# Row sums of the attention by four products of their own, and the router's logits in a bank of their own

## The chip, the cores and the metric

The kernel runs on one core of one Trainium2 chip. The metric is the device time of one execution in microseconds (us); several executions are timed and the median counts. TensorE (PE) runs matrix products and loads their stationary operand by separate records (PEld). VectorE (DVE), ScalarE (ACT) and GpSimd (POOL) do the element work, SyncE (SP) issues most of the DMA transfers. Each engine works through its own instructions in program order and waits on semaphores where it needs another engine's result.

## The reference

Three layers in float32, cut to what matters:

```python
# attention: batch 8, 8 heads, 576 positions, head size 64, in chunks of 64
scores = scale * np.matmul(q_c, k_c.transpose(0, 1, 2, 4, 3))
scores = scores - np.max(scores, axis=-1, keepdims=True)
attn = np.exp(scores)
attn = attn / (np.sum(attn, axis=-1, keepdims=True) + 1e-09)
out = np.matmul(attn, v_c)          # becomes x: 4608 tokens x 512
# mixture of 8 experts, one expert per token
logits = x @ w_gate                 # 512 x 8
expert_idx = np.argmax(logits, axis=1)
out[mask] = gate_w[mask, None] * (np.maximum(xe @ w1[e], 0.0) @ w2[e])
# a dense layer 512 -> 2048 -> 512 with a piecewise function between
```

## The kernel before

The 4608 tokens are 36 tiles of 128 (NT). **Attention** runs as 42 steps (attention_step, L711), a software pipeline over the tiles: in step i PE does, in this order, scores(i) into s (L456, 8 products), transp(i-1) of the exponentials into t (L464, 4), xtransp(i-3) of the finished rows into tx (L484, 4), pv(i-2), the product of the transposed exponentials with v into ob (L476, 8), logits(i-4) by expert into lt (L544, 4) and by_token(i-5) (L551, 1), which turns the logits so that tokens stand on the partitions. A float32 product of the kind used here leaves two records on PE and two on PEld, a transpose one of each. The products s and pv use 64 columns of the array each, two at a time side by side; logits uses 32; by_token and the transposes use all 128.

v comes with a column of ones behind each head's 64 columns (arrange, L1191), so pv gives 2 x 65 columns per pair of heads, and the 65th is the sum of the exponentials. DVE, per step (vector_work, L487): the maximum mx(i) of s (L500), the subtraction into p(i) (L503), then rd(i-2) from the 65th columns (L516), its reciprocal (L518), and the scaled rows xr(i-2) (L520), which xtransp takes up one step later. ACT: the copy pt of t (L491), the copy xc of tx (L495), the exponential of p (L504), the copy lt of the logits (L529). Between these stand small DVE operations of the router's gate (gate, L553), some DVE and ACT work on the first expert's weights (raw to wt, L106, L109, L112), and, from batch 3 of the gate on, the fetch of the first window of rows for the experts (fetch, L184): POOL scatters the tokens' places into lists (L617), gathers a list (L163) and rows xg (L140), DVE takes their maxima (L100).

The order on PE, DVE, ACT and SP is written out by the code: background work is inserted by a planner that adds up fixed costs per step (slot, spend, clk), which the change leaves alone. POOL's order is left to the scheduler of the framework. PSUM has 8 banks of 512 float32 per partition. In the attention they are: s two, t one, tx one, ob three (one tile, the middle bank shared by the even and the odd tiles' results), la one. The bank la holds the logits by expert (columns 256 to 383), the logits by token and the counts of the gate (acc). The framework puts accesses of different engines to one bank in program order by semaphores.

**Experts** (ffn, L919): 16 windows of up to 512 tokens; per window 8 groups of 12 products h (L932) and 24 products per tile y (L966). In window 0, in which the last tiles' gate work still runs on PE (rest_of_gate), the h groups go round three banks (hs, L914); from window 1 on, once the attention's banks are free, round four. Window 1's rows come by a chain of their own after the last batch was counted: lists, gathers, maxima, halves in float16, DMA transposes into xtw. **The dense layer** (L1089 on) is products without a gap, o (L1145) and h (L1117).

Of the kernel before, what the change touches and what calls it, by code (L numbers as in the profile page):

```python
# [8 lines left out]
F32 = mybir.dt.float32  # L9
# [4 lines left out]
ALU = mybir.AluOpType  # L14
# [4 lines left out]
P = 128  # L19
NT = 36  # L20
# [18 lines left out]
AHEAD = 3  # L39
# [15 lines left out]
def build(ctx, tc, qT, kT, v1, wg, w1, w2, wi, wo, out):  # L55
    nc = tc.nc
    pe, act, dve, pool, sp = nc.tensor, nc.scalar, nc.vector, nc.gpsimd, nc.sync
# [10 lines left out]
    with tc.manual_schedule(engines={E_.PE, E_.Activation, E_.DVE, E_.SP}):  # L68
# [46 lines left out]
        early = rows.enter_context(tc.tile_pool(name="early", bufs=1, side="right"))  # L115
# [238 lines left out]
        with ExitStack() as ph:  # L354
# [5 lines left out]
            ps_o = ph.enter_context(tc.tile_pool(name="ps_o", bufs=1, space=PSUM))  # L360

            kbd = [bd.tile([P, 2, 2, 4, 2, 64], F32, name=f"kbd{i}") for i in range(AHEAD)]
            vbd = [bd.tile([P, 2, 2, 4, 2, 65], F32, name=f"vbd{i}") for i in range(AHEAD)]
            qt = {}

            def clear(t, by, n=slice(0, 2)):
# [39 lines left out]
            pool.memset(ones16, 1.0)  # L406
            zero16 = early.tile([P, GB + 1, E], F16, name="zero16")
            pool.memset(zero16, 0.0)
            tri16 = early.tile([P, P], F16, name="tri16")
            pool.memset(tri16, 1.0)  # L410
            pool.affine_select(out=tri16, in_=tri16, pattern=[[1, P]], base=0, channel_multiplier=-1,
# [33 lines left out]
            for t in xgs:  # L445
                pool.memset(t, 0.0)

            S, Pm, PT, O, X, XR, LG = {}, {}, {}, {}, {}, {}, {}
            xr = [None]

# [9 lines left out]
            def transp(i):  # L460
                p = Pm.pop(i)
                t = ps_t.tile([P, 4, P], F32, name="t", tag="t")
                for hp in range(4):
                    pe.transpose(t[:, hp, :], p[:, hp * P:hp * P + P], ident)  # L464
                PT[i] = t


            ob = ps_o.tile([P, 1536], F32, name="ob")
            obs = [ob[:, 0:684].rearrange("p (a c) -> p a c", c=171)[:, :, 0:130],
                   ob[:, 812:1496].rearrange("p (a c) -> p a c", c=171)[:, :, 41:171]]  # L470

            def pv(i):
                pt, vb, o = PT.pop(i), vbd[i // 2 % AHEAD][:, :, i % 2], obs[i % 2]
                for hp in range(4):
                    for c in range(2):
                        pe.matmul(o[64 * c:64 * c + 64, hp, :], lhsT=pt[:, hp, 64 * c:64 * c + 64], rhs=vb[:, :, hp, c, :],  # L476
                                  start=True, stop=True)
                O[i] = o

            def xtransp(i):  # L480
# [6 lines left out]
            def vector_work(i):  # L487

                if 0 <= i - 1 < NT:
                    pt = mid.tile([P, 4, P], F32, name="pt", tag="pt")  # L490
                    act.activation(out=pt, in_=PT[i - 1], func=AF.Copy)  # L491
                    PT[i - 1] = pt
                if 0 <= i - 3 < NT:
                    xc = xcp.tile([P, 4, P], F32, name="xc", tag="xc")
                    act.activation(out=xc, in_=X[i - 3], func=AF.Copy)  # L495
                    X[i - 3] = xc
                if i < NT:
                    s3 = S.pop(i).rearrange("p (h k) -> p h k", k=64)
                    mx = mid.tile([P, H, 1], F32, name="mx", tag="mx")
                    dve.tensor_reduce(out=mx, in_=s3, axis=AX.X, op=ALU.max)  # L500
                    yield
                    p = mid.tile([P, 512], F32, name="p", tag="p", bufs=3)
                    dve.tensor_tensor(out=p.rearrange("p (h k) -> p h k", k=64), in0=s3, in1=mx.to_broadcast([P, H, 64]), op=ALU.subtract)  # L503
                    act.activation(out=p, in_=p, func=AF.Exp, scale=0.125)  # L504
                    Pm[i] = p
                    spend(1.35, 0.55)
                slot(1.15)
                yield
                j = i - 2
                if 0 <= j < NT:  # L510
                    if j % 2 == 0:
                        xr[0] = xrp.tile([P, 2, D], F32, name="xr", tag="xr")
                    x = XR[j] = xr[0][:, j % 2]
                    o4 = O.pop(j).rearrange("p a (h d) -> p a h d", d=65)
                    rd = mid.tile([P, 4, 2, 1], F32, name="rd", tag="rd")
                    dve.tensor_scalar(out=rd, in0=o4[:, :, :, 64:65], scalar1=1e-9, scalar2=None, op0=ALU.add)  # L516
                    yield
                    dve.reciprocal(out=rd, in_=rd)  # L518
                    yield
                    dve.tensor_tensor(out=x.rearrange("p (a h d) -> p a h d", h=2, d=64), in0=o4[:, :, :, 0:64],  # L520
                                      in1=rd.to_broadcast([P, 4, 2, 64]), op=ALU.mult)
                    if j % 2 == 1:
                        sp.dma_start(out=xd[(j - 1) * P:(j + 1) * P, :].rearrange("(p t) d -> p (t d)", p=P), in_=xr[0].rearrange("p t d -> p (t d)"))
                    spend(0.95, 0.5)
                slot(1.15)
                yield
                if 0 <= i - 4 < NT:
                    lt = xcp.tile([P, P], F32, name="lt", tag="lt")
                    act.activation(out=lt, in_=LT[i - 4], func=AF.Copy)  # L529
                    LT[i - 4] = lt  # L530
                    spend(0.0, 0.65)
                slot(1.15)
                yield
# [5 lines left out]
            def logits(i):  # L539

                xc = X.pop(i)
                lt = LT[i] = la[:, 256:384]
                for dc in range(4):
                    pe.matmul(lt[32 * dc:32 * dc + 32, :], lhsT=wgr[:, dc, :], rhs=xc[:, dc, :], start=True, stop=True)  # L544

# [301 lines left out]
        with ExitStack() as ph:  # L847
# [63 lines left out]
            htp = ph.enter_context(tc.tile_pool(name="htp", bufs=1))  # L911
            ps_h = ph.enter_context(tc.tile_pool(name="ps_h", bufs=1, space=PSUM))
            ps_y = ph.enter_context(tc.tile_pool(name="ps_y", bufs=1, space=PSUM))
            hs = [ps_h.tile([P, 512], F32, name=f"h{i}") for i in range(3)]  # L914

            more_ys = []
            ht = htp.tile([P, 2, 8, 512], F16, name="ht")
# [133 lines left out]
            for w, (r, k, size) in enumerate(windows):  # L1051
                final = w == len(windows) - 1
                if k == 0:
                    ready[1] = max(ready[1], 2 * r + 2)
                    if r > 0:
                        ready[0] = r + 2
                more = w + 1 < len(windows) and windows[w + 1][1] == 0

                def beside(t):
                    if w == 0:  # L1060
                        next(rest_of_gate, None)
                    slot(t)

                def after(n):
                    leave_one()
                    if more and n == 8:
                        ready[1] = 2 * r + 3

                while w not in xts:
                    advance()  # L1070
                if 0 < w and not final:
                    background.insert(0, fetch(w + 1))
                xt, ids, gates, inv = xts.pop(w)
                ffn(r, xt, size, ids, gates, inv, beside, after, final, before_last if final else None)
                if w == 0:
                    now(rest_of_gate)
                    ps_h4 = ph.enter_context(tc.tile_pool(name="ps_h4", bufs=1, space=PSUM, side="right"))
                    hs.insert(0, ps_h4.tile([P, 512], F32, name="h3"))
                    more_ys.append(ps_h4.tile([P, 512], F32, name="y3"))
                    mpool = ctx.enter_context(tc.tile_pool(name="mw", bufs=1, side="right"))  # L1080
                    mlpw = mpool.tile([P, 17, 2048], F16, name="mlpw")
                    background.append(load_mlp())
# [95 lines left out]
def arrange(np, q, k, v, w_gate, w1, w2, w_in, w_out):  # L1178
    c = np.ascontiguousarray

    def tiles(x):
        return x.reshape(8, 8, 9, 64, 64).transpose(0, 2, 1, 3, 4).reshape(NT, 2, 4, 2, 64, 64)

    def pairs(x):
        return c(x.reshape(NT // 2, 2, P, -1).transpose(0, 2, 1, 3)).reshape(NT // 2, P, -1)

    def transposed(x):
        return pairs(tiles(x).transpose(0, 3, 5, 2, 1, 4).reshape(NT, P, 512))

    vt = tiles(v).transpose(0, 3, 4, 2, 1, 5)  # L1190
    v1 = np.concatenate([vt, np.ones(vt.shape[:-1] + (1,), v.dtype)], axis=-1)  # L1191
    a = {"qT": transposed(q), "kT": transposed(k), "v1": pairs(v1.reshape(NT, P, 520)),
         "wg": c(w_gate.reshape(4, P, E).transpose(1, 0, 2)).reshape(P, 4 * E)}
    for i in range(4):
        a[f"w1_{i}"] = c(w1[:, i * P:(i + 1) * P, :]).reshape(E * P, 1024)
        a[f"w2_{i}"] = c(w2.reshape(E, 4, 2, P, D)[:, i].transpose(0, 2, 1, 3)).reshape(E * P, 1024)
    a["w_in"] = c(w_in.reshape(4, P, 2, 1024).transpose(0, 2, 1, 3)).reshape(8, P, 1024)
    a["w_out"] = c(w_out.reshape(8, 2, P, D).transpose(0, 2, 1, 3)).reshape(8, P, 1024)
    if a["w_in"].dtype == np.float64:
        a["w_in"], a["w_out"] = a["w_in"].view(np.int64), a["w_out"].view(np.int64)  # L1200
    return a
```

## Time and profile before

| | us |
|---|---|
| median of 3 runs | 1379.84 (1378.0 to 1382.45) |
| the profiled execution, its own time | 1387.27 |
| its span in the trace | 1385.3 |
| PE busy in the span | 1325.9 (96%) |
| attention, first product to the first product of window 0 | 4.89 to 189.85 |
| window 0, until PE starts window 1 | 189.85 to 233.36 |
| all the rest | 233.36 to 1385.3 |

The profiled execution is 7.4 us above the median. A busy PE is one with a product under way; gaps stand in brackets behind an instruction, with what ended them. "Issue" is a gap that no semaphore explains. The granted clock of PE is 1.00 for 2.4 GHz and 0.50 for 1.2 GHz.

### The profile page before, as it was taken

The numbers are of one execution on the slowest core, as the hardware profiler recorded it, in microseconds if no ns is written. First come the engines' busy times: TensorE is split into PE (matmuls) and PEld (weight loads), VectorE is DVE, ScalarE is ACT, GpSimd is POOL, SyncE is SP. The second block draws the span as 40 slices with busy tenths as digits, with TensorE's granted clock in tenths as the row PEclk, the third lists the DMA queues.
The fourth block names the chain that finished last, engine by engine and source line by source line (L and its number), as shares of the span: only waits on it lengthen the run. The fifth ranks groups of instructions, "written<-read, shape, count | busy, mean of one in ns | idle before, by whom it ended". The sixth has DMA issues, their size and how long they took to land.

```text
span 1385.3 us, 20006 instructions
## 1 busy us (share of the span) xinstructions
PE 1325.9 (96%) x7735; PEld 697.8 (50%) x7735; DVE 766.2 (55%) x1545; ACT 593.9 (43%) x1000; POOL 151.9 (11%) x190
## 2 busy tenths in 40 slices
PE   7888788999999999989999999999999999999998
PEld 5666653445445445555444444444444444444555
DVE  5558655678678777756464270724518064370723
ACT  3446433666666766644242240413315042240522
POOL 3111231221231222310000000000000000000000
PEclk9999899999999999999999999999999999999999
DMA  9989636666667663312111111111110111111000
GB/s 242 286 265 279 161 91 197 206 206 232 192 204 239 174 207 109 98 52 77 31 53 31 62 22 35 35 31 61 31 61 1 31 61 31 54 23 37 22 26 16
DMA packets 123201, 147.99 MB, mean 107 GB/s; under 512 B 89164, under 2 KB 89164, under 8 KB 121056
## 3 DMA queue, kind: packets, MB, share of 16 engines
q1 hardware_dynamic: 115264, 127.40, 32.6%
q0 software_dynamic: 7840, 19.29, 4.1%
q8 instruction: 62, 1.02, 0.3%
q14 instruction: 35, 0.29, 0.1%
HBM read 99.10 MB, written 29.72 MB: 93 GB/s over the span
## 4 chain that ended last, share of the span: by engine, by line
PE 55%; ACT 0%; issue 0%
PE h L1117 27%; PE o L1145 27%; PE y L966 1%; ACT y L954 0%; ACT ot L1138 0%
## 5 line engine op out<-in xcount | busy, mean ns | idle before, releaser
L1117 PE MATMUL h<-xtw,mlpw 128*128 128x512 f16 (+2 forms) x1920 | 375.1, 358 | 0.8 <-ACT y L954 0.8
L1145 PE MATMUL o<-mlpw,gt 128*128 128x512 f16 x1728 | 374.6, 379 | 0.0
L1122 DVE SCALAR_TENSOR_TENSOR q<-r,kf_g 128x512 f32<-128x512 f32 (+2 forms) x160 | 111.7, 698 | 363.7 <-ACT r L1120 363.7
L1117 PEld LDWEIGHTS <-mlpw 128*128 128x128 f16 x1920 | 187.8, 98 | 187.0 <-issue 1.1
L1145 PEld LDWEIGHTS <-gt 128*128 128x128 f16 x1728 | 169.2, 98 | 203.3
L932 PE MATMUL h<-xtw,wt 128*128 128x384 f16 (+2 forms) x1248 | 213.5, 332 | 14.5 <-DMA xtw<-xh 9.9
L966 PE MATMUL y<-wt,ht 128*128 128x512 f16 x960 | 212.2, 383 | 5.6 <-DVEq L994 5.6
L1120 ACT ACTIVATE r<-h,b_g,a_g 128x512 f32<-128x512 f32 (+2 forms) x160 | 117.6, 735 | 184.9 <-PE h L1117 182.4
L932 PEld LDWEIGHTS <-wt 128*128 128x128 f16 x1248 | 122.4, 99 | 103.6 <-DMA xtw<-xh 10.9
L966 PEld LDWEIGHTS <-ht 128*128 128x128 f16 x960 | 94.5, 99 | 120.0 <-issue 9.6
L1138 ACT ACTIVATE ot<-o,io_g 128x512 f32<-128x512 f32 x36 | 24.0, 688 | 289.7 <-PE o L1145 283.6
L1123 DVE SCALAR_TENSOR_TENSOR q<-h,c_g,q 128x512 f32<-128x512 f32 (+2 forms) x160 | 111.7, 698 | 5.7
L1110 DVE TENSOR_TENSOR gt<-q,gt 128x512 f16<-128x512 f32 (+2 forms) x160 | 100.6, 629 | 1.1 <-ACT gt L1109 0.2
L1109 ACT ACTIVATE gt<-q 128x512 f16<-128x512 f32 (+2 forms) x160 | 92.2, 576 | 10.2 <-DVE q L1123 10.2
L112 DVE SCALAR_TENSOR_TENSOR wt<-raw,s_w,wt 128x1024 f16<-128x1024 f32 x64 | 79.4, 1278 | 8.5 <-ACT wt L109 8.5
L109 ACT ACTIVATE wt<-raw,s_w 128x1024 f16<-128x1024 f32 x64 | 70.5, 1139 | 31.6 <-DVE i_w L89 25.5
L938 DVE SCALAR_TENSOR_TENSOR ht<-h,ht 128x384 f16<-128x384 f32 (+2 forms) x104 | 58.3, 562 | 43.7 <-ACT ht L937 42.1
L106 ACT ACTIVATE wt<-raw 128x1024 bf16<-128x1024 f32 x64 | 66.9, 1048 | 5.1 <-DMA raw<-w 5.1
L937 ACT ACTIVATE ht<-h 128x384 f16<-128x384 f32 (+2 forms) x104 | 50.3, 491 | 43.2 <-PE h L932 37.0
L958 POOL DMA_INDIRECT yd<-y,list x40 | 42.2, 1055 | 92.5 <-ACT y L954 84.8
L456 PE MATMUL s<-kbd,qt 128*64 128x128 f32 x576 | 44.9, 303 | 6.6 <-DMA kbd<-kT 6.5
L476 PE MATMUL ob<-vbd,pt 128*64 128x130 f32 x576 | 45.7, 296 | 5.2 <-issue 5.2
(160 smaller groups left out, 907.4 us busy)
## 6 DMA issues: line engine op xcount, KB each, us to landing
raw<-w SPq DMA_DIRECT2D x64, 512.0 KB
vbd<-v SPq DMA_DIRECT2D x36, 260.0 KB
xd<-xr SPq DMA_DIRECT2D x18, 512.0 KB
xg<-yd SPq DMA_DIRECT2D x36, 256.0 KB
out<-ot SPq DMA_DIRECT2D x36, 256.0 KB
qt<-qT SPq DMA_DIRECT2D x16, 512.0 KB
kbd<-kT SPq DMA_DIRECT2D x32, 256.0 KB
mlpw<-w_in SPq DMA_DIRECT2D x8, 1024.0 KB
```

The costliest lines, as they stand in the source:

```text
L106: act.activation(out=junk, in_=src, func=AF.Square, accum_out=ss)
L109: act.activation(out=hi, in_=src, func=AF.Copy, scale=s)
L112: dve.scalar_tensor_tensor(out=lo, in0=src, scalar=s, in1=hi, op0=ALU.mult, op1=ALU.subtract)
L932: pe.matmul(h[:, 0:N], lhsT=wa[:, a, wc:wc + P], rhs=xt[:, 4 * b + dc, 0:N], start=n == 0, stop=n == 11)
L966: pe.matmul(ys[t], lhsT=ht[:, a, f, c0 + t * P:c0 + (t + 1) * P], rhs=wb[:, b, f * D:(f + 1) * D], start=f == 0 and n == 0, stop=f == 7 an ...
L1109: act.activation(out=gt[:, 0, f, 0:N], in_=q, func=AF.Copy)
L1110: dve.tensor_tensor(out=gt[:, 1, f, 0:N], in0=q, in1=gt[:, 0, f, 0:N], op=ALU.subtract)
L1117: pe.matmul(h[:, 0:N], lhsT=w_in(a, dc, f), rhs=yt[:, 4 * b + dc, 0:N], start=n == 0, stop=n == 11)
L1120: act.activation(out=r, in_=h[:, 0:N], func=AF.Relu, scale=ci["a"], bias=ci["b"])
L1122: dve.scalar_tensor_tensor(out=q, in0=r, scalar=ci["sq"], in1=r, op0=ALU.min, op1=ALU.mult)
L1123: dve.scalar_tensor_tensor(out=q, in0=h[:, 0:N], scalar=ci["c2"], in1=q, op0=ALU.mult, op1=ALU.max)
L1145: pe.matmul(os_[t], lhsT=gt[:, a, f, t * P:(t + 1) * P], rhs=w_out(b, f), start=f == 0 and n == 0, stop=f == 15 and n == 2)
```

## The change

v loses its column of ones: pv has 128 columns per pair of heads, vbd and the input array shrink by 1/65, and ob becomes two tiles of one bank each. The sums come from four new float32 products per tile, right behind pv in the same step: lhsT is the transposed exponentials of two heads (128 x 128), rhs a constant of_head of two columns (ones for the first head's 64 rows, ones for the second's). Their eight results per row lie in a new bank lb, in one of two places by the tile's parity, and rd reads them there. The logits by expert, lt, move from la into lb too; la keeps the logits by token and the counts. The attention's 8 banks are then s two, t, tx, ob two, la, lb; so window 0 of the experts has two h banks where it had three, and four from window 1 on as before. POOL gets three small memsets for of_head at the start.

```diff
-            vbd = [bd.tile([P, 2, 2, 4, 2, 65], F32, name=f"vbd{i}") for i in range(AHEAD)]
+            vbd = [bd.tile([P, 2, 2, 4, 2, 64], F32, name=f"vbd{i}") for i in range(AHEAD)]
...
+            of_head = early.tile([P, 2], F32, name="of_head")
+            pool.memset(of_head, 0.0)
+            for i in range(2):
+                pool.memset(of_head[64 * i:64 * i + 64, i:i + 1], 1.0)
...
-            ob = ps_o.tile([P, 1536], F32, name="ob")
-            obs = [ob[:, 0:684].rearrange("p (a c) -> p a c", c=171)[:, :, 0:130],
-                   ob[:, 812:1496].rearrange("p (a c) -> p a c", c=171)[:, :, 41:171]]
+            obs = [ps_o.tile([P, 4, P], F32, name=f"ob{i}") for i in range(2)]
+
+            lb = ps_l.tile([P, 512], F32, name="lb")
...
                     for c in range(2):
                         pe.matmul(o[64 * c:64 * c + 64, hp, :], lhsT=pt[:, hp, 64 * c:64 * c + 64], rhs=vb[:, :, hp, c, :],
                                   start=True, stop=True)
+                dn = RS[i] = lb[:, P + i % 2 * 8:P + i % 2 * 8 + 8].rearrange("p (a h) -> p a h", h=2)
+                for hp in range(4):
+                    pe.matmul(dn[:, hp, :], lhsT=pt[:, hp, :], rhs=of_head, start=True, stop=True)
                 O[i] = o
...
-                    o4 = O.pop(j).rearrange("p a (h d) -> p a h d", d=65)
+                    o4 = O.pop(j).rearrange("p a (h d) -> p a h d", d=64)
                     rd = mid.tile([P, 4, 2, 1], F32, name="rd", tag="rd")
-                    dve.tensor_scalar(out=rd, in0=o4[:, :, :, 64:65], scalar1=1e-9, scalar2=None, op0=ALU.add)
+                    dve.tensor_scalar(out=rd, in0=RS.pop(j).unsqueeze(3), scalar1=1e-9, scalar2=None, op0=ALU.add)
...
-                lt = LT[i] = la[:, 256:384]
+                lt = LT[i] = lb[:, 0:P]
...
-            hs = [ps_h.tile([P, 512], F32, name=f"h{i}") for i in range(3)]
+            hs = [ps_h.tile([P, 512], F32, name=f"h{i}") for i in range(2)]
...
-                    hs.insert(0, ps_h4.tile([P, 512], F32, name="h3"))
+                    for i in (2, 3):
+                        hs.insert(0, ps_h4.tile([P, 512], F32, name=f"h{i}"))
```

The orders of PE, DVE, ACT and SP stay as they were but for the new products; what changes beside them is what waits for what. In the rows below a name like DVE_49 in the brackets is the semaphore of that engine. On PE, one step in the middle of the attention, before:

```order
L484 MATMUL tx<-ident,xr 128x128 [waits DVE_49,PE_49]
L484 MATMUL tx<-ident,xr 128x128 x3
L476 MATMUL ob<-vbd_132,pt 64x130 [waits DMAHW4_49,DMAHW3_49]
L476 MATMUL ob<-vbd_132,pt 64x130 x7
L544 MATMUL la<-xc,wgr 32x128 [waits Activation_49]
L544 MATMUL la<-xc,wgr 32x128 x3
L551 MATMUL la<-sel_205,lt 128x8
```

and the same step now:

```order
L491 MATMUL tx<-ident,xr 128x128 [waits DVE_49,PE_49]
L491 MATMUL tx<-ident,xr 128x128 x3
L480 MATMUL ob_232<-vbd_132,pt 64x128 [waits DMAHW4_49,DMAHW3_49]
L480 MATMUL ob_232<-vbd_132,pt 64x128 x7
L484 MATMUL lb<-of_head,pt 128x2 [waits Activation_49]
L484 MATMUL lb<-of_head,pt 128x2 x3
L551 MATMUL lb<-xc,wgr 32x128 x4
L558 MATMUL la<-sel_209,lt 128x8
```

Four products stand between pv and the logits, and the wait for ACT's copy of the last tile's logits has moved from the logits to the first of them.

On DVE, the end of a step with a gate's first operations, and the next step's start, before:

```order
L516 TENSOR_SCALAR rd<-ob 128x8 [waits PE_49]
L518 RECIPROCAL rd<-rd 128x8 [waits DVE_49]
L520 TENSOR_TENSOR xr<-ob,rd 128x512 [waits DMAHW3_49,DVE_49]
L557 TENSOR_REDUCE m<-la 128x6 [waits Activation_49]
L560 TENSOR_TENSOR eq<-la,m 128x48 [waits DVE_49]
```

and now:

```order
L523 TENSOR_SCALAR rd<-lb 128x8 [waits PE_49,Activation_49]
L525 RECIPROCAL rd<-rd 128x8 [waits DVE_49]
L527 TENSOR_TENSOR xr<-ob_232,rd 128x512 [waits DMAHW3_49,DVE_49]
L564 TENSOR_REDUCE m<-la 128x6 [waits PE_49]
L567 TENSOR_TENSOR eq<-la,m 128x48 [waits DVE_49]
```

rd waited for the last product of pv; now it waits for the last product of the logits in the same step (they write lb behind the sums) and for ACT's copy of the step before. m, the gate's maximum, waited for ACT's copy lt in the same bank and now waits for PE alone. In turn ACT's copy lt, which waited for PE, waits for DVE's rd.

On ACT, window 0 of the experts, the first copies of h, whose numbers tell the banks, before:

```order
L937 ACTIVATE ht<-h_2428 128x384 [waits PE_49]
L937 ACTIVATE ht<-h_2429 128x384 [waits PE_49]
L937 ACTIVATE ht<-h_2427 128x384 [waits PE_49]
L937 ACTIVATE ht<-h_2428 128x384 [waits PE_49]
L106 ACTIVATE wt,ss<-raw 128x1024 [waits DMAHW7_49]
```

and now:

```order
L944 ACTIVATE ht<-h_2578 128x384 [waits PE_49]
L944 ACTIVATE ht<-h_2577 128x384 [waits PE_49]
L944 ACTIVATE ht<-h_2578 128x384 [waits PE_49]
L944 ACTIVATE ht<-h_2577 128x384 [waits PE_49]
L106 ACTIVATE wt,ss<-raw 128x1024 [waits DMAHW7_49]
```

Every second group of products now goes into a bank that was read just before, where it was every third.

## Rows read from the trace of the kernel before

**Rows 1.** Busy by stage: us; PE, PEld, DVE, ACT, POOL (records); clock, DMA share, GB/s

```profile
29.24:156.16 126.92, 110.61 (x1398) 86.89 (x1399) 80.62 (x230) 66.48 (x134) 26.81 (x28) 0.97 0.94 268
...
233.36:1385.30 1151.94, 1136.16 (x5688) 557.71 (x5688) 621.76 (x1131) 490.49 (x798) 95.31 (x98) 0.99 0.29 85
```

**Rows 2.** Timeline of one attention step: start us, us, engine, line, tile, count

```profile
75.70 1.09 PE L456 MATMUL s<-kbd,qt 128*64 128x128 f32 x16
...
76.72 0.66 PE L464 MATMUL t<-ident,p 128*128 128x128 f32 x4
...
77.11 0.47 PEld L484 LDWEIGHTS tx<-ident,xr 128*128 128x128 f32 x4
...
77.75 1.11 PE L476 MATMUL ob<-vbd,pt 128*64 128x130 f32 x16
...
78.78 0.42 PE L544 MATMUL la<-xc,wgr 128*32 128x128 f32 x8
78.90 0.17 DVE L516 TENSOR_SCALAR rd<-ob 128x8 f32<-128x8 f32 x1 [0.57 <-PE ob L476]
...
79.14 0.30 PEld L551 LDWEIGHTS la<-sel,lt 128*128 128x128 f32 x2 [0.20 <-issue]
...
79.34 0.69 DVE L520 TENSOR_TENSOR xr<-ob,rd 128x512 f32<-128x512 f32 x1
...
79.46 1.09 PE L456 MATMUL s<-kbd,qt 128*64 128x128 f32 x16
```

**Rows 3.** Timeline, float16 weight loads of the gate's count on PEld

```profile
86.59 0.22 PEld L578 LDWEIGHTS <-tri 128*128 128x128 f16 x6
...
86.74 0.22 PEld L580 LDWEIGHTS <-ones 128*128 128x128 f16 x6
```

**Rows 4.** Line L551 and line L484: duration ns min/median/max, first and last start

```profile
L551 PEld LDWEIGHTS la<-sel,lt x72: 186/189/338, 28.6 to 195.6; 128*128 128x128 f32 x72
...
L484 PEld LDWEIGHTS tx<-ident,xr x144: 137/141/231, 20.2 to 190.7; 128*128 128x128 f32 x144
```

**Rows 5.** Waits of PE from 16 to 190 us: in total, times, longest

```profile
PE t L464 <- ACT p L504: 9.5, 5, 6.0
PE ob L476 <- issue: 5.2, 8, 1.0
PE la L544 <- DVE eq L565: 3.4, 1, 3.4
PE tx L484 <- DVE xr L520: 2.4, 3, 1.9
...
PE s L456 <- DMA kbd<-kT: 0.2, 1, 0.2
```

**Rows 6.** Waits of DVE and ACT up to 240 us: in total, times, longest

```profile
DVE xr L520 <- DMA xd<-xr: 5.3, 4, 2.9
...
ACT wt L106 <- DMA raw<-w: 5.1, 2, 4.8
```

**Rows 7.** Timeline of PE: batch 3 counted, and the longest wait, with its neighbours

```profile
134.22 0.24 PE L580 MATMUL la<-oh,ones 128*128 128x32 f16 x4
...
156.16 1.13 PE L456 MATMUL s<-kbd,qt 128*64 128x128 f32 x16
163.32 1.12 PE L464 MATMUL t<-ident,p 128*128 128x128 f32 x4 [6.03 <-ACT p L504]
```

**Rows 8.** Stretches at the lower clock in the attention, columns as in Rows 1

```profile
87.14:90.55 3.41, 3.41 (x24) 2.88 (x22) 3.21 (x12) 2.39 (x5) 0.00 (x0) 0.50 1.01 240
158.82:172.47 13.65, 9.15 (x73) 7.42 (x73) 11.51 (x38) 4.62 (x10) 1.01 (x1) 0.50 0.34 55
```

**Rows 9.** Timeline of PE: window 0 of the experts and the start of window 1

```profile
206.85 4.06 PE L932 MATMUL h<-xtw,wt 128*128 128x384 f16 x24 [1.61 <-DVE ht L938]
210.75 15.70 PE L966 MATMUL y<-wt,ht 128*128 128x512 f16 x72
233.36 17.71 PE L932 MATMUL h<-xtw,wt 128*128 128x384 f16 x96 [6.91 <-DMA xtw<-xh]
```

More of the change, by code (lines that the diff above doesn't have):

```diff
@@ L446, in build @@
                 pool.memset(t, 0.0)
+            RS = {}
             S, Pm, PT, O, X, XR, LG = {}, {}, {}, {}, {}, {}, {}
@@ L519, in vector_work @@
                     yield
-                    dve.tensor_tensor(out=x.rearrange("p (a h d) -> p a h d", h=2, d=64), in0=o4[:, :, :, 0:64],
+                    dve.tensor_tensor(out=x.rearrange("p (a h d) -> p a h d", h=2, d=64), in0=o4,
                                       in1=rd.to_broadcast([P, 4, 2, 64]), op=ALU.mult)
@@ L1190, in arrange @@
     vt = tiles(v).transpose(0, 3, 4, 2, 1, 5)
-    v1 = np.concatenate([vt, np.ones(vt.shape[:-1] + (1,), v.dtype)], axis=-1)
-    a = {"qT": transposed(q), "kT": transposed(k), "v1": pairs(v1.reshape(NT, P, 520)),
+    a = {"qT": transposed(q), "kT": transposed(k), "v1": pairs(vt.reshape(NT, P, 512)),
          "wg": c(w_gate.reshape(4, P, E).transpose(1, 0, 2)).reshape(P, 4 * E)}
```

## Prediction

> **What bounds the kernel now.** I read the busy time by stage first. From 233 us to the end PE is busy 1136.2 of 1151.9 us [rows 1], so whatever the change does there is nothing unless it adds products, and it adds none; a delay made before 233 us is carried to the end whole. The change is in the attention. There, from 29 to 156 us, PE is busy 110.6 of 126.9 us, while DVE has 80.6 and ACT 66.5 [rows 1]: PE is the bound, with gaps. The timeline of one step says the same in another way: scores start at 75.70 and again at 79.46, and the blocks in between follow each other [rows 2]. A step that nothing disturbs is 3.76 us of PE, in order. The DMA engines are busy 0.94 of that stage [rows 1], yet PE waits for a load itself for only 0.2 us after the start [rows 5]; the loads run far enough ahead. So the question is what four more products per tile cost on PE, and how much of it falls into gaps that are there anyway.
>
> **The new products.** Each of the four leaves two loads of 128 x 128 float32 weights, and only two columns to stream behind each, so the loads set the pace. The nearest row is by_token, one product of the same weight shape with 8 columns: its two loads take 0.30 us together [rows 2] and one takes 0.189 [rows 4], so the second starts 0.11 us after the first. The four transposes tx, 128 columns each, give the same: 0.47 us for four loads [rows 2] of 0.141 each [rows 4], (0.47 - 0.14) / 3 = 0.11. Eight loads are 0.88 us. Behind a block of another tile shape there is a break: by_token's start at 79.14 to the next scores at 79.46 is 0.32 = 2 x 0.11 + 0.10 [rows 2]. The change makes one more such border (64 to 128 columns, 128 to 32, instead of 64 to 32), so 0.10. Per tile 0.98 us, and 36 tiles make **35.3 us**. From both sides: the transposes t start 0.39 us ahead of tx [rows 2] for four, 0.10 each or a little under, so 0.09 per load as the low end, 8 x 0.09 + 0.10 = 0.82, 29.5 us; by_token's whole 0.32 for two loads as the high end, 0.16 per load, 1.28, 46 us. I take 0.98, since by_token and tx agree on it.
>
> **What pv gives back.** Two columns of 130. The pv block takes 77.75 to 78.78, 1.03 us, the scores block with 128 columns 75.70 to 76.72, 1.02 us [rows 2]: 0.01 per tile, 0.4 us in all. DVE's xr reads the same 512 elements; I give it nothing. Bytes of v fall by 1/65; as PE does not wait for loads, nothing either, as long as it doesn't.
>
> **What of it falls into gaps.** Gross it is 35.3 - 0.4 = 34.9 us. PE's gaps from 16 to 190 us: the big groups are 9.5 us for the exponentials p, 3.4 for the gate's eq, 2.4 for xr, and 5.2 without a releaser ("issue") [rows 5]. The last I leave: nothing in the change feeds PE its instructions sooner. The others end by chains on DVE, ACT or DMA that do not get longer by the new products, so a PE that arrives 0.98 us per step later waits less.
> - p, without its longest wait: 9.5 - 6.0 = 3.5 us in four waits [rows 5]. A chain from scores to p is DVE and ACT work, and PE comes for p a whole step later, now 0.98 us later. I take 3.5 as gone.
> - xr: 2.4 in three [rows 5]; DVE had to wait for the write of older rows to land [rows 6], which was issued some three steps before. Three steps are 2.9 us longer. Gone. (That rd now starts later is weighed as a rival.)
> - eq: 3.4 us, once [rows 5]. ACT stood in a weight square that waited for its load [rows 6], lt behind it, m behind lt in the bank la, and PE behind m. m no longer waits for lt, but the first new product still waits for lt. By one and a half steps between the load's issue and this point, 1.5 us; with the detour by m gone, some more. I take 2.5.
> - The 6.03 us wait at 163.32 [rows 7]. Batch 3 is counted at 134.2; from there lists, gathers and DVE's maxima of the gathered rows, which stand ahead of tile 32's mx on DVE. Five steps and one scores block lie between on PE, so PE comes 5 x 0.98 = 4.9 us later, less the 2 us of short waits in those steps that are gone as counted above. The chain itself is POOL and DMA, and keeps its length. I take 3 of the 6.
> - Smaller ones and the start: 0.6.
>
> Together 3.5 + 2.4 + 2.5 + 3 + 0.6 = **12 us**. At least: 8, if the two long waits stay. At most: 16 (all but "issue" of the rows 5, with the small ones), and the stretch at the lower clock after the eq wait, 3.4 us at 0.50 [rows 8], costs 1.7 us that would go too.
>
> **Window 0 with two banks.** A group of products now has to wait for the copy of the group before last. In the trace PE waited 1.6 us there with three banks; with two I'd add up to 2 us. But PE ends window 0 at 226.4 and waits until 233.36 for window 1's rows [rows 9], by a chain that starts when the last batch is counted, in the third group of eight, before any bank comes round to a late copy. So 6.9 us cover it; without that cover it would be those 2 us.
>
> **The sum.** 35.3 - 0.4 - 12 = +22.9 us. The profiled execution took 1387.27, which would become 1410; it was 7.4 above the median, and I put the same difference on the median: 1379.84 + 22.9 = **1403 us**, slower by 1.7%. The ends: low 29.5 - 0.4 - 16 - 1.7 = +11, 1391; high 46 - 0.4 - 8 = +38, 1417.
>
> **Rivals.**
> *Cheap products.* If weight loads in front of two columns went at the pace of the gate's count, six in 0.15 us (86.59 to 86.74) [rows 3], 0.025 each, a tile would cost 8 x 0.025 + 0.10 = 0.30, 36 tiles 10.8, less 0.4 and some 10 us of gaps: **1380**, no change. The Trainium skill (TensorE: Matmul & The Clock Gate, section Back-to-back issue gap) gives about 25 ns as the floor for products of up to 64 columns, which would make it so. But its section LDWEIGHTS (loading the stationary operand) gives columns / 1.2 in ns, 107 ns for 128 columns, and this trace agrees with that one for float32 (0.11) and with the first for float16 alone. Against the rival speaks by_token, the same dtype and shape. 6%.
>
> *The loads were the brake.* With DMA at 0.94 [rows 1], a shorter v could let late data come sooner: the waits behind data, xr 2.4, eq 3.4 and the one of 6.0 [rows 5], would vanish, 11.8 us, and with them the stretches at the lower clock behind them, 3.4 and 13.65 us at 0.50 [rows 8], which cost half their length, 8.5. That is 20 us, and it decides only where the products cost less than 20 us in all, so together with the cheap pace: 10.4 - 20 = -10, **1370**, faster. Against it: 1/65 of a third of the bytes is little. 4%.
>
> *The bank lb as a chain.* rd waited for pv, ending by 78.78; it started at 78.90, and xr ended at 79.34 + 0.69 = 80.03, 1.13 after rd's start [rows 2]. Now rd waits for the logits behind the new products. From the logits' end PE needs 0.32 (by_token), 1.02 (scores), 0.5 (t) until it asks for xr: 1.84 us against 0.12 + 1.13 = 1.25. So 0.6 us are left, and as long as DVE comes to rd in time the new wait costs nothing. A weight cast or gate operations ahead of rd on DVE make it late; where that is 1.3 us, PE loses 0.7. In some 25 steps of 36 that would be 18 us on top: **1421**. The Trainium skill (PSUM — Partial Sum Buffer, section PSUM bank collisions raise a hardware error) says that two engines may not use one bank at once even at different columns, which is why the waits stand in the order. The trace shows such a chain once, in eq's 3.4 us. 8%.
>
> **How the numbers follow.** The forecast has 82%, and its own range, 1391 to 1417, holds nearly all of that; the cheap pace 6%, the faster case 4%, the chain 8%. 18% lie outside, plus a little of the forecast's own, so the range stays 1391 to 1417. About 0.3%, 4 us, is what a measurement of this kernel can tell from no change. Slower by more: 82 + 8 = 90%. Within: 6%. Faster: 4%.
>
> **What would show it.** In the changed kernel's profile: 288 records of the new products on PEld, 0.11 us from one start to the next, a block of about 1 us between pv and the logits; undisturbed steps of 4.7 us instead of 3.76; the first product of window 0 at about 212 instead of 190, window 1 at about 256 with a wait of some 5 to 7 us before it, and the same 1152 us after that. Among PE's waits that for p falls to about 3 us, that for xr and eq to near nothing. The prediction is wrong if the block is 0.3 us, if waits for xr appear in most steps, or if the gaps swallow more than 16 us.

## The result, and the profile after

The changed kernel takes 1395.78 us (median of 4 runs, 1389.24 to 1396.12), beside 1378.92 for the kernel before in the same comparison (1372.58 to 1382.45). The ratio is 1.0116, with a 95% interval of 1.0068 to 1.0164: it is **slower by 16.9 us**, 1.2%, and the interval stands for 9 to 23 us. The forecast was slower by 22.9 us, 1403, so the measured time lies in its range and the forecast's own difference just past the upper end of that interval. The profiled execution of after took 1396.11 us with a span of 1394.4.

Of the page of after, the busy times. The line of TensorE says where the time went: PE was busy 1325.9 us before, in 96% of its span, and PE's loads now have 288 records more than the 7735 of before.

```profile
PE 1355.0 (97%) x8023; PEld 728.9 (52%) x8023; DVE 767.0 (55%) x1545; ACT 594.0 (43%) x1000; POOL 152.7 (11%) x193
```

The timeline of PE for one step of after that nothing disturbs, as [rows 2] showed one of before (line numbers moved: scores L461, transposes of p L469, xtransp L491, pv L480, the sums L484, logits L551, by_token L558):

```profile
150.60 1.09 PE L461 MATMUL s<-kbd,qt 128*64 128x128 f32 x16
151.63 0.66 PE L469 MATMUL t<-ident,p 128*128 128x128 f32 x4
152.12 0.60 PE L491 MATMUL tx<-ident,xr 128*128 128x128 f32 x4
152.65 1.09 PE L480 MATMUL ob<-vbd,pt 128*64 128x128 f32 x16
153.67 1.05 PE L484 MATMUL lb<-of_head,pt 128*128 128x2 f32 x8
154.66 0.42 PE L551 MATMUL lb<-xc,wgr 128*32 128x128 f32 x8
155.01 0.39 PE L558 MATMUL la<-sel,lt 128*128 128x8 f32 x2
155.33 0.44 PE L461 MATMUL s<-kbd,qt 128*64 128x128 f32 x4
```

The new block runs from 153.67 to 154.66, 0.99 us; the step from 150.60 to 155.33, 4.73 us, where it was 3.76.

The waits of PE in the attention of after, from 16 us on, to be held against [rows 5]:

```profile
PE tx L491 <- DVE xr L527: 2.0, 3, 0.9
PE t L469 <- ACT p L511: 1.7, 1, 1.7
PE lb L484 <- ACT lt L536: 0.6, 1, 0.6
```

Three kinds and 4.3 us are left; the 9.5 for p are 1.7, eq's 3.4 are gone, and so is every gap of the kind "issue".

Last, the three stages of after by their busy times (columns as in [rows 1]): attention from its first product to the first product of window 0, window 0 up to the start of window 1, and the rest; and, in a second fence, the first two of the profiled execution that the forecast was made from.

```profile
4.99:195.30 190.31, 181.49 (x2123) 152.04 (x2124) 117.06 (x316) 86.21 (x173) 44.63 (x76) 0.96 0.80 227
195.30:241.82 46.52, 36.20 (x213) 18.94 (x214) 25.18 (x95) 15.93 (x29) 12.96 (x14) 0.90 0.44 127
241.82:1394.40 1152.58, 1137.34 (x5688) 557.86 (x5688) 621.71 (x1129) 490.62 (x798) 94.57 (x98) 0.99 0.29 85
```

```profile
4.89:189.85 184.96, 155.26 (x1835) 122.18 (x1836) 117.05 (x317) 86.32 (x172) 43.98 (x73) 0.93 0.85 233
189.85:233.36 43.51, 34.46 (x215) 17.93 (x214) 24.49 (x93) 15.78 (x29) 12.08 (x13) 0.97 0.43 131
```

The rest is 1152.58 against 1151.94 [rows 1]: as forecast, nothing happens behind 242 us. But the attention is only 5.35 us longer than in that execution, where 22 were expected. PE's gaps in it, the time less the busy time, fell from 184.96 - 155.26 = 29.7 to 190.31 - 181.49 = 8.8 us. So either the gaps swallowed far more than the forecast allowed, or that execution of before was a poor one to start from. The first run was made to tell this.

### The profile page after: what moved, and what is told of

Same layout as the page of the kernel before. It is cut to its first block, busy times and chain, and to the rows that moved or that the text cites. A ratio compares the mean times of both kernels' runs of the same rounds, so it can differ in the third digit from the quotient of the medians.

```text
span 1394.4 us, 20596 instructions
## 1 busy us (share of the span) xinstructions
PE 1355.0 (97%) x8023; PEld 728.9 (52%) x8023; DVE 767.0 (55%) x1545; ACT 594.0 (43%) x1000; POOL 152.7 (11%) x193
## 4 chain that ended last, share of the span: by engine, by line
PE 54%; ACT 0%; issue 0%
PE h L1125 27%; PE o L1153 27%; PE y L973 1%; ACT y L961 0%; ACT ot L1146 0%
## 5 line engine op out<-in xcount | busy, mean ns | idle before, releaser
L939 PE MATMUL h<-xtw,wt 128*128 128x384 f16 (+2 forms) x1248 | 216.7, 335 | 15.0 <-DMA xtw<-xh 12.4
L140 POOL DMA_INDIRECT xg<-xd,list x40 | 44.0, 1100 | 63.5 <-DMA list<-ld,li 30.8
L624 POOL DMA_INDIRECT ld<-tok,slot x36 | 36.3, 1009 | 132.3 <-DVE slot L622 74.3
```

Source lines behind the costliest of these rows:

```text
L939: pe.matmul(h[:, 0:N], lhsT=wa[:, a, wc:wc + P], rhs=xt[:, 4 * b + dc, 0:N], start=n == 0, stop=n == 11)
```

## Experiments

Each comparison has its own runs of the kernel before on the same chip; ratios are against those.

**1. The kernel before, once more.**

> The kernel before once more, for a second trace of it. The changed kernel was 16 us slower, 35 us of products less some 18 us that must have fallen into gaps; in its trace the gaps without a releaser (issue) on TensorE, 9.1 us in the first trace of before, are gone altogether. If such gaps belong to the kernel before, a second trace has some 5 to 10 us of them again, between 16 and 190 us; if the first trace was a chance, it has under 2 us. The time should be 1379, ratio 1.00.

Measured: 1378.14 us (10 runs, 1371.72 to 1383.66), ratio 1.0007 [0.9987, 1.0028]. The profiled execution is the fastest of these, 1371.72. Its attention and window 0, and its waits of PE in the attention, here from 16 to 170 us (one more for xr, of 0.6 us, follows before window 0):

```profile
5.60:172.82 167.22, 144.02 (x1836) 115.01 (x1836) 116.06 (x314) 85.79 (x172) 45.31 (x73) 0.95 0.92 257
172.82:216.31 43.49, 33.90 (x214) 18.02 (x214) 24.93 (x97) 15.83 (x29) 12.02 (x13) 0.94 0.42 132
```

```profile
PE t L464 <- ACT p L504: 9.4, 8, 5.6
PE la L544 <- DVE eq L565: 3.2, 1, 3.2
PE la L544 <- ACT lt L529: 2.7, 1, 2.7
PE tx L484 <- DVE xr L520: 2.4, 2, 1.9
PE s L456 <- DMA kbd<-kT: 0.5, 1, 0.5
PE la L544 <- DVE base L601: 0.5, 1, 0.5
```

The same program has no "issue" gap at all here, and its attention takes 167.22 us instead of 184.96, with as many records (1836 loads in each). The waits for p and eq are those of [rows 5] to 0.2 us and those for xr to 0.6, with one of 2.7 for lt on top: they belong to the kernel. The "issue" gaps do not come with the program, and neither do 11.2 us of PE's busy time (part of that is the clock, 0.93 there and 0.95 here). After's attention is 23.1 us longer than this one. The sum by terms, against this execution: 36 x 0.97 = 34.9 for the products; PE's gaps 23.2 to 8.8, so -14.4; together 20.5. The other 2.6 are left over; the mean clock, 0.95 here and 0.96 in after, does not explain them.

**2. After without the four products** (rd reads the first column of ob; the sums are left out):

```diff
-                dn = RS[i] = lb[:, P + i % 2 * 8:P + i % 2 * 8 + 8].rearrange("p (a h) -> p a h", h=2)
-                for hp in range(4):
-                    pe.matmul(dn[:, hp, :], lhsT=pt[:, hp, :], rhs=of_head, start=True, stop=True)
...
-                    dve.tensor_scalar(out=rd, in0=RS.pop(j).unsqueeze(3), scalar1=1e-9, scalar2=None, op0=ALU.add)
+                    dve.tensor_scalar(out=rd, in0=o4[:, :, :, 0:1], scalar1=1e-9, scalar2=None, op0=ALU.add)
```

> The changed kernel without its four products: the sums of the exponentials are left out, and rd reads the first column of the result of v in their place. All else of the change is in (v without ones, two banks of ob, logits in lb). Theory 1 (the gaps went because TensorE comes later in every step): without the products the gaps are back, and the time is that of before, 1379 (1375 to 1383). Theory 2 (the gaps went because of v's shorter rows or the separate banks): they stay away and the time is 1379 less some 18, 1361 (1357 to 1367).

Measured: 1431.2 us (1428.99 to 1432.18), ratio 1.0376 [1.0358, 1.0393]. A miss of the experiment, not of a theory. Rows divided by arbitrary numbers give other logits, so the tokens spread over the experts in another way, and the experts do more work: PE has 5808 records behind the start of window 1 instead of 5688 [rows 1], and in one stretch of 54 us it is busy for only 14.7 (columns as in [rows 1]).

```profile
606.00:660.00 54.00, 14.69 (x119) 9.80 (x120) 20.37 (x53) 21.36 (x34) 11.14 (x12) 0.59 0.25 84
218.40:1430.50 1212.10, 1155.26 (x5808) 568.72 (x5808) 641.36 (x1183) 511.38 (x832) 106.76 (x111) 0.97 0.29 85
```

Nothing on the products follows from its time. It was made again as run 3.

**3. The same, with a constant for the sum** (left out: the sums; every row is divided by the same 30, and DVE's operation is the same but for its operands). Inputs drawn as the reference draws them give sums of some 62 in every row, so x is about twice its value, and the order of a token's logits hardly changes:

```diff
+                    dve.tensor_scalar(out=rd, in0=o4[:, :, :, 0:1], scalar1=0.0, scalar2=30.0, op0=ALU.mult, op1=ALU.add)
```

> The changed kernel without its four products, as e1, but with the sum of the exponentials replaced by the constant 30, written by the same DVE operation, so that the experts get nearly their usual shares (e1 read a wrong number there and ended after the overflow loop had work). The sums are left out. Theory 1 (the gaps come back when TensorE is faster): about the time of before, 1374 to 1382, and PE's waits for p, eq and xr add up to 14 us or more again. Theory 2: under 1368.

Measured: 1375.75 us (10 runs, 1368.72 to 1380.43 and one of 1550.3), ratio 0.9967 [0.9938, 0.9995]. PE has 5688 records behind the start of window 1, as before. With all else of the change in place and only the products out, the kernel is at the time of before or 0.3% under it. The waits of PE are back:

```profile
PE t L469 <- ACT p L508: 10.2, 6, 6.9
PE lb L548 <- ACT lt L533: 10.0, 2, 7.6
PE tx L488 <- DVE xr L524: 3.5, 4, 1.9
PE s L461 <- DMA kbd<-kT: 1.0, 1, 1.0
```

24.7 us of waits against after's 4.3: without the products PE comes earlier and waits 20 us more. That is what the products take back in this layout of the banks; 34.9 - 20.4 leaves 14.5 us of price, and the time says somewhat more (next run). Before's layout gives less back: 7.6 us of the 24.7 are a single wait for lt, in whose place run 1 has one of 2.7 for lt and one of 3.2 for eq.

**4. Before, with the four products added** into columns of la that nobody reads:

```diff
+                dn = la[:, 448:456].rearrange("p (a h) -> p a h", h=2)
+                for hp in range(4):
+                    pe.matmul(dn[:, hp, :], lhsT=pt[:, hp, :], rhs=of_head, start=True, stop=True)
```

> The kernel before with the four products alone: v keeps its ones, rd reads the sums there, and the products' results lie unread in spare columns of la. If the price is the products', it is as slow as the changed kernel, 1393 to 1400. If the new banks or v's shape cost or gave something, the difference to the changed kernel shows it: over 1402 if they gave, under 1390 if they cost.

Measured: 1393.8 us (1389.2 to 1398.99), ratio 1.0123 [1.0094, 1.0151]. That is the whole change's price to 0.1%, with no other part of it. In the same comparison run 3 took 1375.75: the products cost 18 us net of what the gaps take back. Its waits of PE in the attention sum to 5.2 us (3.8 for p, 0.9 for eq, 0.5 for lt), so it is the products that fill the gaps, not the new banks.

**5. After with v's 65 columns loaded as before** (pv reads 64 of them):

```diff
+            vbd = [bd.tile([P, 2, 2, 4, 2, 65], F32, name=f"vbd{i}") for i in range(AHEAD)]
...
+                        pe.matmul(o[64 * c:64 * c + 64, hp, :], lhsT=pt[:, hp, 64 * c:64 * c + 64], rhs=vb[:, :, hp, c, 0:64],
```

> The changed kernel with v's column of ones loaded as before (260 KB in place of 256 per tile and transfer row of 4160 bytes), of which the products use 64 columns. Theory 1 (pace): the same time as the changed kernel, 1396 (1392 to 1400), and no gaps without a releaser. Theory 2 (v's rows): such gaps return, 9 us and the low clock behind them, 1405 to 1414.

Measured: 1394.68 us (1393.85 to 1395.02), ratio 1.0116 [1.0099, 1.0133], the ratio of after. The shorter rows of v are worth nothing that can be measured; the rival that the loads were the brake falls.

**6. After with the products issued twice:**

```diff
+                for hp in range(8):
+                    pe.matmul(dn[:, hp % 4, :], lhsT=pt[:, hp % 4, :], rhs=of_head, start=True, stop=True)
```

> The changed kernel with each of the four products of the sums issued twice into the same place. With nearly no gaps left to fall into (5 us of waits in the changed kernel's attention) the second four show their price: 8 loads of 0.11 us, 0.88 per tile, 31.7 us for 36, less up to 4 us of waits: 1396 + 28 to 32 = 1424 to 1428. If the price were 0.025 a load: 1396 + 7 = 1403. If the chain through the bank lb set the step's length, more than 1428.

Measured: 1457.08 us (1454.58 to 1463.57), ratio 1.0582 [1.055, 1.0614]. The price of a block is right and the total is not. A step of PE, and then stretches of 3.4 us (columns as in [rows 1]):

```profile
125.30 1.95 PE L484 MATMUL lb<-of_head,pt 128*128 128x2 f32 x16
127.18 0.42 PE L551 MATMUL lb<-xc,wgr 128*32 128x128 f32 x8
```

```profile
90.52:93.93 3.41, 3.41 (x44) 3.12 (x42) 1.18 (x4) 0.91 (x2) 2.50 (x4) 1.00 0.99 286
93.93:97.35 3.42, 3.42 (x26) 2.77 (x24) 2.46 (x8) 1.64 (x3) 2.81 (x3) 0.50 0.94 260
97.35:100.76 3.41, 3.41 (x42) 3.00 (x41) 0.48 (x3) 0.36 (x2) 0.05 (x1) 1.00 0.02 2
100.76:104.17 3.41, 3.41 (x24) 2.75 (x22) 2.18 (x6) 0.92 (x2) 0.00 (x0) 0.50 0.37 115
...
18.84:264.60 245.76, 243.47 (x2394) 207.50 (x2391) 115.11 (x323) 87.64 (x173) 36.82 (x41) 0.81 0.57 163
```

125.30 to 127.18 is 1.88 us for 16 loads, 0.89 more than the block of after. But the granted clock is 0.50 in every second of these stretches, although PE is busy from end to end in all four; over the 245.76 us it is 0.81. A stretch at 0.50 loses at most half its length, so a mean of 0.81 is up to 0.19 x 245.76 = 46.7 us lost to the clock, where after, with 0.96 over the 190.31 us of its attention, lost up to 7.6. The 29 to 33 us by which the total passes the expectation lie within that difference of 39. So that the clock is their cause is an estimate that fits, not something taken apart by a run.

**7. After with the sums by DVE** (a reduction of p over each head's 64 columns, no products; the whole result):

```diff
+                    Pm[i] = RS[i] = p
...
+                    dve.tensor_reduce(out=rd.rearrange("p a h o -> p (a h) o"), in_=RS.pop(j).rearrange("p (h k) -> p h k", k=64), axis=AX.X, op=ALU.add)
+                    yield
+                    dve.tensor_scalar(out=rd, in0=rd, scalar1=1e-9, scalar2=None, op0=ALU.add)
```

> The changed kernel with the sums taken by DVE from p (one reduction of 0.69 us per tile) in place of the four products; all else as in the changed kernel. TensorE's step is 3.75 us again. DVE was busy 81 of 127 us in the attention and gets 25 us more in all. If that fits into its waits, the time is that of before, 1374 to 1380. If DVE becomes late for p and xr, 1382 to 1392. Under 1370 would beat both kernels.

Measured: 1382.54 us (1377.83 to 1386.3), ratio 1.0022 [1.0004, 1.0039]. Its reductions take 36 x 0.675 = 24.3 us of DVE, which is not the bound:

```profile
L520 DVE TENSOR_REDUCE rd<-p x36: 674/675/681, 18.4 to 183.1; 128x8 f32<-128x512 f32 x36
```

PE then waits for xr eleven times, but 6.5 us in all. In the same comparison run 4, with the sums on PE, took 11 us more (1393.8), since DVE has room in the attention [rows 1] and PE has little. Against run 3, which has no sums at all, some 7 of the 24.3 us show, so not all of them are hidden.

**8. The logits back in la, twice.** One line: lt lies beside the counts again, so rd doesn't wait for the logits, and m and the logits wait as before.

```diff
-                lt = LT[i] = lb[:, 0:P]
+                lt = LT[i] = la[:, 256:384]
```

> The changed kernel with the logits by expert back in the bank la; the sums keep lb for themselves, so rd waits for the four products and not for the logits behind them. If the shared bank cost time (rd late, xr late), this is faster than the changed kernel by some us (under 1390). If rd's later start was covered, as the trace of the changed kernel with its three short waits for xr says, it is the same or up to 3 us slower, since the gate's maximum waits for lt again: 1394 to 1399.

Measured: 1390.0 us (1388.27 to 1392.87), ratio 1.0078 [1.0057, 1.0100], 0.4% under after's ratio, from another comparison. So both were run side by side, on another chip, on which the kernel before took some 12 us more (1390.57):

> The changed kernel once more, beside e9 on the same chip. 1395 (ratio 1.012).

> The kernel of e4 once more (logits by expert back in la, the sums alone in lb), beside the changed kernel on the same chip: e4 came out at 1390, 5 us under the changed kernel of an earlier hour. If the shared bank lb costs some 5 us, this is 1390 beside 1395 again, with intervals apart; if that was chance, both have the same ratio to within 0.2%.

Measured: after 1417.01 us (1413.63 to 1423.92), ratio 1.0203 [1.017, 1.0236]; with lt in la 1407.37 (1402.19 to 1414.63), ratio 1.0143 [1.0111, 1.0176]. The two are 9.6 us, 0.6%, apart, and their intervals just overlap. Neither is what was expected: here after is 26.4 us slower than before, not 16.9, so the price of the change itself is not the same in every comparison. By its profile, after's attention has 18 us of gaps here where it had 8.8, and a clock of 0.91 where it had 0.96 (columns as in [rows 1]):

```profile
5.03:215.76 210.73, 192.68 (x2123) 159.30 (x2124) 117.52 (x316) 87.08 (x173) 44.64 (x76) 0.91 0.74 204
```

The waits of DVE for rd show the bank lb at work, first in after, then with lt in la, each in its first comparison:

```profile
DVE rd L523 <- PE lb L551: 49.6, 29, 4.2
```

```profile
  PE lb L484: 41.9, 31
```

In after DVE stands 49.6 / 29 = 1.71 us in front of rd, until the logits (L551) are done; with lt in la 41.9 / 31 = 1.35, until the sums (L484) are. On PE this comes out as waits for xr: 2.0 in after, 0.6 with lt in la in its first comparison. That is a microsecond or two, not five to ten. In the second pair the profiled executions differ by more than this: after's has a stretch of 23.9 us at the lower clock behind a 2.3 us wait for xr (put down to rd, just ahead of it on DVE); the other has a mean clock of 0.57 from 176 to 188 us and 1.00 from there to window 0.

```profile
196.91 0.63 PE L491 MATMUL tx<-ident,xr 128*128 128x128 f32 x4 [2.32 <-DVE rd L525]
```

```profile
197.50:221.40 23.90, 23.01 (x151) 17.15 (x151) 10.94 (x33) 6.40 (x13) 0.28 (x1) 0.50 0.17 56
```

That rd, at 195.64, began more than 2 us behind the last of the logits, with DVE idle for 5.15 us before it, so this wait is no clean case of the bank. And run 4, which has no bank lb at all, costs as much as after. Two comparisons point to 0.4 to 0.6% for the bank, run 4 to nothing; it stays open.

**9. Before, with the first window's rows planned 6 us later.** In run 1 DVE stands 6.46 us in front of the maxima of gathered rows that have not come, and mx and p of the next tile come behind them; PE waits for that p:

```profile
150.19 1.37 DVE L100 TENSOR_REDUCE xam<-xg 128x1 f32<-128x512 f32 x2 [6.46 <-DMA xg<-xd,list]
153.59 0.69 PE L464 MATMUL t<-ident,p 128*128 128x128 f32 x2 [5.59 <-ACT p L504]
```

The planner can be told so:

```diff
-            at = [clk["pool"] + ROWS - 1.05 * (size - 1 - t) for t in range(size)]
+            at = [clk["pool"] + ROWS + (0.0 if w else 6.0) - 1.05 * (size - 1 - t) for t in range(size)]
```

> The kernel before, with the planner told that the first window's gathered rows come 6 us later, so that DVE's maxima of them stand two steps further back. In every trace with TensorE at its old pace, TensorE waits 5 to 7 us for p behind these maxima, and the low clock follows. If that wait is what the four products partly hid, it goes here without any product: 1378 less 5.5 for the wait and some 3 for the clock, 1369 to 1373, which beats both kernels. If the rows' chain comes due somewhere later instead (window 0's first product), 1376 to 1380.

Measured: 1385.98 us (12 runs, 1381.2 to 1390.08) where before took 1390.57, ratio 0.9971 [0.995, 0.9993]. The long wait is in three pieces:

```profile
170.31 0.66 PE L464 MATMUL t<-ident,p 128*128 128x128 f32 x4 [1.12 <-ACT p L504]
173.94 0.66 PE L464 MATMUL t<-ident,p 128*128 128x128 f32 x4 [0.82 <-ACT p L504]
176.93 0.63 PE L484 MATMUL tx<-ident,xr 128*128 128x128 f32 x4 [2.33 <-DVE xr L520]
```

Faster by 0.3%, less than expected; by this trace part of the wait came up again as one for xr (there is no trace of before on this chip to set beside it). It has the lowest ratio of all kernels here that compute the whole result, below both before and after; but with an upper end of 0.9993, and at the 0.3% that the prediction took as the least one can tell, the gain is hardly clear of none.

## Why the prediction held, step by step

**The price of the products: right.** 0.98 us a tile was forecast from by_token and tx, and the block takes 0.99, the step 4.73 instead of 3.76. Twice the products take 1.88, so eight more loads are 0.89, 0.111 each. The low end (0.82) and the high end (1.28) can go. The Trainium skill (TensorE: Matmul & The Clock Gate, section LDWEIGHTS (loading the stationary operand)) gives 107 ns for a load of 128 columns; the 0.111 us agree with it, and not with the 25 ns of the section Back-to-back issue gap, by which the rival of cheap products would have come to 0.30.

**That the products are the price: shown.** Alone in the kernel before they cost 1.23%, the whole change 1.16%; without them the rest of the change costs nothing. For the 2.0% of the later comparison (run 8) it is not shown, since the products alone were not run there.

**What falls into gaps: right in sum on the rows it was made from, too small on the kernel.** On the first execution of before the waits with a releaser went from 16.1 us (9.5, 3.4, 2.4 and three of 0.2 to 0.3) to 4.3, which is 11.8, where 12 was forecast. By terms: p gave 7.8 where 6.5 was expected (3.5, and 3 of the 6.03 us wait; what remains of that one is 1.75), eq gave 3.4 for 2.5, and xr gave 0.4 for 2.4. The xr waits stayed where rd waits for the logits (2.0); in run 4, where it doesn't, there are none. That the sum came out near 12 is in part luck, since the errors of the terms cancel. The least that the gaps were to give, 8, doesn't follow from the prediction's own terms either: without the two long waits 3.5 + 2.4 + 0.6 = 6.5 are left, which would put the upper end at 1419. Against the second execution the gaps gave 14.4.

**"Issue" left standing, and the offset: the step that failed.** The forecast kept those gaps (5.2 us in [rows 5], 9.3 with the smaller groups of that view), and kept the profiled execution's 7.4 us above the median as an offset that before and after share. Run 1 shows an execution of before without these gaps, so they were not to be taken for a property of the kernel; they are also large enough to be the 7.4 us, though that is not shown. After's profiled execution, 0.3 us from its median, has neither. On the profiled run the forecast said 1410 and 1396.11 came; on the median it said +22.9 and +16.9 came.

By its span after's profiled execution is 1394.4 - 1385.3 = 9.1 us longer than the first of before and 1394.4 - 1369.9 = 24.5 longer than the second, which lies 6.4 us under its own median. So how much slower after is depends on the execution of before that it is held against; the 22.9, worked out on the first, lies near what the second gives, and that is luck. By the prediction's own sign, gaps that swallow more than 16 us, its account was too small: 34.9 less the measured 16.9 is 18, of which the waits with a releaser show 11.8 and all of PE's gaps, against the second execution, 14.4. The rest is open.

Whether the products also swallow such gaps where they occur isn't settled: in the attention the first profiled execution of after and those of runs 4, 5 and 6 have none, but neither have those of runs 1 and 3, without the products; on the slower chip of run 8 after, lt in la and run 9 all had some. They may go with the chip.

**Window 0 with two banks: hidden, as forecast.** PE waits 8.64 us for window 1's rows, 6.9 before [rows 9] and 8.94 in run 1:

```profile
241.82 1.46 PE L939 MATMUL h<-xtw,wt 128*128 128x384 f16 x4 [8.64 <-DMA xtw<-xh]
```

The forecast of 256 for this point, and of 212 for window 0's first product, was counted from the first execution, which came to window 0 at 189.85 where run 1 came at 172.82; 241.82 and 195.30 came. Window 0 is 3 us longer all the same, of which the clock, 0.50 in its first 5 us, makes some 2.5 by an estimate (half of 195.30 to 200.41):

```profile
183.34:200.41 17.07, 16.18 (x109) 11.69 (x108) 8.04 (x28) 3.27 (x8) 0.41 (x1) 0.50 0.16 62
```

That it is not the two banks, runs 3 and 4 show by their window 0 (columns as in [rows 1]): run 3, with two, takes 43.26 us, no more than before, and run 4, with three, 45.95.

```profile
178.25:221.51 43.26, 34.11 (x214) 18.01 (x214) 24.80 (x97) 15.81 (x29) 12.02 (x13) 0.95 0.41 131
191.44:237.39 45.95, 33.78 (x214) 18.13 (x214) 24.44 (x93) 15.95 (x29) 12.98 (x14) 0.89 0.43 128
```

**The bank lb as a chain: there, and smaller than the rival's price.** 0.6 us of slack held in most steps; xr made PE wait 3 times, not in 25 steps of 36. The 18 us did not come. Between nothing and 10 us, what it costs is open (run 8).

## What to carry to other kernels

These products, with two columns behind each load, were priced by their weight loads; read the load's pace from a neighbour of the same dtype and shape, and multiply. The two large groups of gaps with a releaser (p and eq) came back in the next execution to 0.2 us, and they swallowed new work; the gaps without one did not come back in it, so look at a second execution before a sum is built on one that has them. An engine with room beside the bound was the cheaper place for the sums: against before they cost 0.2% on DVE and 1.2% on PE.

## What the hardware showed that was not expected

The granted clock fell while PE was busy without a break (run 6). In after it happened once in the middle of the attention, with PE nearly always busy but for a wait of 0.56 us that ended at 108.96 (columns as in [rows 1]):

```profile
105.00:111.66 6.66, 6.10 (x79) 5.09 (x77) 3.66 (x9) 3.08 (x7) 0.29 (x1) 1.00 1.05 344
111.66:115.07 3.41, 3.41 (x24) 3.08 (x24) 1.60 (x8) 0.83 (x1) 0.38 (x1) 0.50 1.01 257
```

With the products doubled it happened in every second stretch of run 6 shown above, with no wait in them: 2.4 GHz, 1.2, 2.4, 1.2, at a busy share of 1.00. What PE did in the stretch before a fall was, among other blocks, the one of 16 loads with two columns behind each (97.77 to 99.64 before the fall at 100.76). The Trainium skill (TensorE: Matmul & The Clock Gate, section What's actually happening) says that activity is what releases the throttle; in these rows the clock fell with PE busy by its records throughout, and here the measurement decides. Why it fell, these runs don't tell. By the estimate under run 6 it cost some 30 us there, about as much as the second set of products itself, 36 x 0.89 = 32 us at full clock.
